# Router products of one more block on TensorE, expert weights split four slots ahead, output scaling on VectorE

## The chip, the cores and the metric

The kernel runs on one core of a Trainium2 chip. The metric is the device time of one execution in microseconds (us), lower is better. In the profile PE is TensorE (PEld its weight loads), DVE is VectorE, ACT is ScalarE, POOL is GpSimd and SP is the engine that only issues transfers.

## The reference

Three layers follow each other on 2304 tokens of 512 features, all in fp32. First comes a linear attention of 4 batches with 8 heads each, which produces the tokens. The second layer is a dense pair of products with a leaky relu, 512 to 2048 and back to 512. The third, where the change lies, sends every token to one of eight experts:

```python
logits = xn @ en.T / tau            # xn, en: rows of x and of expert_emb, normalised
expert_idx = np.argmax(logits, axis=1)
probs = softmax(logits)             # with 1e-9 in the sum
gate_w = probs[np.arange(N), expert_idx]
for e in range(E):
    mask = expert_idx == e
    h = np.maximum(x[mask] @ w1[e], 0.0)      # 512 -> 1024
    out[mask] = gate_w[mask, None] * (h @ w2[e])   # 1024 -> 512
```

## The kernel before

**Precision.** A product in fp32 is made of three passes: each operand is split into a rounded part `hi` (a cast on ScalarE) and the rest `lo` (a subtraction), and hi*hi, hi*lo and lo*hi are added up in PSUM.

**Dense layer.** Tokens are worked in nine blocks of 256 (j = 0 to 8), twice: a first pass with half of the 2048 hidden features, together with the attention, and a second pass (`mm1`, `mm2`) with the other half. After a block's second pass `y_half_b(j)` (L564) adds both halves to `ys` on VectorE, stores the rows, and needs the products of each row with the eight expert embeddings. For j < `J_PE` these are 16 reductions over 512 elements on VectorE (L582, two row tiles by eight experts, with the embeddings `enb` held broadcast in SBUF). For j >= `J_PE`, only j = 8 before, TensorE transposes the rows (L593), ScalarE copies them (L595), and TensorE multiplies them with the embeddings (L601). `route(j)` then picks the expert and counts ranks with many small VectorE operations and four small matmuls (L631, L632).

**Lists.** The tokens of one expert are gathered in tiles of 128. Five early tiles (0 to 4) are listed from the first twelve row tiles, while the dense layer is still running. The late list (`make_list`, `list_ids`, `list_tail`) needs block 8's routing; its VectorE work runs while the early tiles are computed, and its matmuls stand at fixed places of the steps: ranks (L632) at the start of step 2, counts (L680) in step 2, ids (`pp`, L754) in step 3, gates (L781) in step 5.

**Expert steps.** Step i computes tile i in four slots. Slot 0 is the first half of the up product (`up(i, 0)`, L901 to L905), slot 1 the first half of the down product of tile i-1 (`down(i-1, 0)`, L931 to L935) and the transposes of tile i's hidden values (`hT(i, 0)`, L915), slots 2 and 3 the second halves. ScalarE takes the relu of an up product (`hs`, L908) and casts the transposed values (`h`, L918), and `hT` can't start before `hs`. TensorE keeps the written order in all steps. In steps 0 and 1 (`I_ACT`) ScalarE keeps the written order too. Elsewhere a scheduler places the instructions ahead of time by priority and by its own estimate of when each is ready, and each engine then runs them in that fixed order.

**Weights.** An expert's weights are four chunks of 1 MB, c = 0 to 3, each with one buffer `raw[c]`. `split(k)` (L841) makes the pair of slot k: `whi` by two casts of 1024 columns on ScalarE (L856), `wlo` by two subtractions (L858), on VectorE but for the second half of c = 3, and of c = 2 in tiles 0 to 2 (`I_POOL`, `C_POOL`), which go to GpSimd. After it, GpSimd issues the load of the next tile's chunk into `raw[c]` (L816), only where the expert changes. Pair k is split in program order `LEAD` = 2 slots before its use. There is room for six pairs: four in `ring_b` (the room of the dense layer's weights W8 to W15, free as block 8's second product uses them up), one in `xb` (the room of two blocks' inputs) and one in `ring_c` (the room of `enb`, free once the last product on VectorE is done). Which pool a pair takes goes by its place modulo six (L845).

**Output.** `finish(i)` (L937) scales a tile's result by its gate on ScalarE (L940, out of PSUM) and GpSimd scatters the rows to the output (L941). The last two of 25 possible tiles stand under a condition that is not met here: 23 run.

Of the kernel before, what the change touches and what calls it, by code (L numbers as in the profile page):

```python
# [15 lines left out]
AF = mybir.ActivationFunctionType  # L16
ALU = mybir.AluOpType
# [19 lines left out]
N_PLAIN = 23  # L37
BIG = 8192.0
PRIO = 1000
J_PE = 8  # L40
J_UP = 9
W_DVE = ()
N_TOP = 2
# [16 lines left out]
MAN = (mybir.EngineType.PE,)  # L60
ENDS = (0, 1)
TAILS = ((1, 1), (1, 2), (2, 0), (2, 1))
I_POOL = (0, 1, 2)
C_POOL = (2,)


# [1 line left out]
def tile_attention_moe_router_experts(ctx, tc, qT, kT, va, w_phi, moew, emb, embT, tau, ew, out):  # L68
    nc = tc.nc
# [9 lines left out]
    def bc(ap, shape):  # L79
        return ap.to_broadcast(shape)  # L80
# [18 lines left out]
    for i in range(2):  # L99
        for r in range(2):  # L100
            nc.vector.tensor_copy(
                out=wblk[r * D:(r + 1) * D, i, r * F:(r + 1) * F],
                in_=wstk[r * D:(r + 1) * D, i, :].bitcast(F32),
# [373 lines left out]
    def b_load(j):  # L477
# [23 lines left out]
        out=upper, in_=upper, pattern=[[1, P]], compare_op=ALU.is_gt, fill=0.0, base=0, channel_multiplier=-1  # L501
# [4 lines left out]
    def iota_f(shape, pattern, base_, cm, name):  # L506
# [16 lines left out]
        out=lt8, in0=bc(io8.unsqueeze(2), [P, NE, NE]),  # L523
# [40 lines left out]
    def y_half_b(j):  # L564
        yt = ypt.pop(j)
        on_pe = j >= J_PE
        yss = []
# [226 lines left out]
    def gather(i):  # L794
        xgt = m1.tile([P, DM], F32, tag="xgt", name="xgt")
        nc.gpsimd.indirect_dma_start(
            out=xgt, out_offset=None, in_=y_d[0:T_EARLY * P, :] if i < N_EARLY else y_d,
            in_offset=bass.IndirectOffsetOnAxis(ap=lists[i][1], axis=0),
        )
        xgs[i] = xgt  # L800

    def xT(i):
        xgt = xgs.pop(i)
        ps = ps_t.tile([P, DM], F32, tag="t", name="xtp")
        for k in range(4):
            nc.tensor.transpose(ps[:, k * P:(k + 1) * P], xgt[:, k * P:(k + 1) * P], ident)
        x = m1.tile([P, 2, 4, P], F32R, tag="xt", name="xt")
        with tc.high_priority(offset=200):
            nc.scalar.copy(out=x[:, 0], in_=ps)
            nc.vector.tensor_sub(  # L810
                x[:, 1].rearrange("q k t -> q (k t)"), ps, x[:, 0].rearrange("q k t -> q (k t)").bitcast(F32)
            )
        xt[i] = x
# [10 lines left out]
    def load_w(i, c):  # L824
        if i == 0 or i >= N_PLAIN:
            load_rows(i, c)
            return
        if i not in need:
            need[i] = nc.values_load(
                lists[i][2], engines=[mybir.EngineType.Pool], min_val=0, max_val=3 * NE  # L830
            )
        with tc.If(need[i] < NE):
            load_rows(i, c)

    def chunk_of(k):
        i, s = divmod(k, 4)
        return ((i, 0), (i - 1, 2), (i, 1), (i - 1, 3))[s]
# [3 lines left out]
    def split(k):  # L841
        i, c = chunk_of(k)
        if not span[0] <= i < span[1]:
            return
        n = (k - 2 if k > 3 else k // 2) % 6  # L845
        if n == 2:
            pool, tag = xg, "xb"
        elif n == 5:
            pool, tag = ring_c, "W"
        else:  # L850
            pool, tag = ring_b, "W"
        hi = pool.tile([P, 2048], F32R, tag=tag, name="whi")
        lo = pool.tile([P, 2048], F32R, tag=tag, name="wlo")
        for h in range(2):
            hs_ = slice(h * 1024, (h + 1) * 1024)
            nc.scalar.copy(out=hi[:, hs_], in_=raw[c][:, hs_])  # L856
            eng = nc.gpsimd if h == 1 and (c == 3 or (i in I_POOL and c in C_POOL)) else nc.vector
            eng.tensor_sub(lo[:, hs_], raw[c][:, hs_], hi[:, hs_].bitcast(F32))  # L858
        wt_[i, c] = (hi, lo)
        if i + 1 < span[1]:  # L860
            load_w(i + 1, c)
# [60 lines left out]
    yacc = {}  # L922
# [14 lines left out]
    def finish(i):  # L937
        oi, gt = tails[i]
        o = xg.tile([P, DM], F32, tag="w32", name="o", bufs=3)
        nc.scalar.activation(out=o, in_=yacc.pop(i), func=AF.Copy, scale=gt)  # L940
        nc.gpsimd.indirect_dma_start(  # L941
            out=out, out_offset=bass.IndirectOffsetOnAxis(ap=oi, axis=0), in_=o, in_offset=None,
            bounds_check=NTOK - 1, oob_is_err=False,
        )

    LEAD = 2

    def step(i, t0, t1, at):
        live, prev, more = i < t1, i > t0, i + 1 < t1
        at(i, 0)  # L950
        if 4 * i + LEAD > 3:
            split(4 * i + LEAD)
        if more:
            gather(i + 1)
        if live:
            up(i, 0)
        at(i, 1)
        split(4 * i + 1 + LEAD)
        if prev:
            down(i - 1, 0)  # L960
        if live:
            hT(i, 0)
        at(i, 2)
        split(4 * i + 2 + LEAD)
        if live:
            up(i, 1)
        if more:
            xT(i + 1)
        at(i, 3)
        split(4 * i + 3 + LEAD)  # L970
        if prev:
            down(i - 1, 1)
            finish(i - 1)
        if live:
            hT(i, 1)

    def run(t0, t1, at=lambda i, n: None):
        span[:] = [t0, t1]
        for i in range(t0, t1 + 1):
            lead = tc.manual_schedule(engines={mybir.EngineType.Activation}) if i in I_ACT else nullcontext()  # L980
            with lead:
                step(i, t0, t1, at)
# [35 lines left out]
    with tc.If(live_rv > N_PLAIN - N_EARLY):  # L1018
        span[:] = [N_PLAIN, N_TILES]
        gather(N_PLAIN)  # L1020
        for c in range(4):
            load_w(N_PLAIN, c)
        xT(N_PLAIN)
        split(4 * N_PLAIN)
        with tc.manual_schedule(engines=set(MAN)):
            run(N_PLAIN, N_TILES)

# [46 lines left out]
```

## Time and profile before

| | |
|---|---|
| median of 3 runs | 945.04 us (941.79 to 949.37) |
| profiled execution | 945.95 us, span 944.1 us |
| busy: PE, DVE, ACT, POOL | 889.6 (94%), 681.5 (72%), 567.1 (60%), 349.2 (37%) us |
| DMA | 120.67 MB, 128 GB/s over the span |
| stages | attention and first pass to about 415, second pass to 621, expert steps from 616 to 930 |

The span is from the first to the last instruction; the execution's own time is 1.85 us longer. TensorE's matmuls overlap in the records, so a stretch with PE busy throughout can still hide small stalls; the waits are read from the idle time in brackets.

### The profile page before, as it was taken

How to read it: one execution, taken by the hardware profiler on the slowest of the kernel's cores; microseconds unless marked ns; L12 is line 12 of the kernel's file. 1: busy time of each engine (PE TensorE's matmuls, PEld its weight loads, DVE VectorE, ACT ScalarE, POOL GpSimd, SP SyncE). 2: the span in 40 equal slices, each digit the busy share in tenths (PEclk: the TensorE clock that was granted, in tenths of full speed). 3: DMA queues.
4: the chain of work that ended last, by engine and by line, in shares of the span. 5: the costliest groups of instructions: out<-in, count | busy, mean ns of one | idle time of the engine just before them, and what ended most of it. 6: DMA issues, size and time to landing. Idle time of an engine off the chain costs nothing. (4 is left out here: it accounts for less than half of the span.)

```text
span 944.1 us, 18507 instructions
## 1 busy us (share of the span) xinstructions
PE 889.6 (94%) x7104; PEld 758.7 (80%) x7104; DVE 681.5 (72%) x1337; ACT 567.1 (60%) x1032; POOL 349.2 (37%) x269
## 2 busy tenths in 40 slices
PE   7889999999999899879999999997889999999994
PEld 5678888888898788779888889886678887888873
DVE  5676547475654544656888889999998888898860
ACT  5876647485555544753333333476788987888861
POOL 1321203032020321562223334426664576554650
PEclk9999999999999999999999999999899999999997
DMA  8773414223030212872222224401551469311650
GB/s 257 245 236 107 140 38 136 94 72 115 25 114 31 84 67 74 270 261 90 90 91 90 90 90 141 184 34 61 192 194 45 160 209 352 136 41 35 227 187 6
DMA packets 43756, 120.67 MB, mean 128 GB/s; under 512 B 4686, under 2 KB 23246, under 8 KB 36624
## 3 DMA queue, kind: packets, MB, share of 16 engines
q1 hardware_dynamic: 33424, 61.48, 19.8%
q0 software_dynamic: 10160, 57.94, 17.6%
q8 instruction: 57, 0.93, 0.4%
q14 instruction: 35, 0.29, 0.1%
q10 hardware_dynamic: 80, 0.03, 0.0%
HBM read 95.84 MB, written 24.90 MB: 128 GB/s over the span
## 5 line engine op out<-in xcount | busy, mean ns | idle before, releaser
L354 PE MATMUL y<-W,gg 128*128 128x512 f32 x864 | 232.3, 402 | 8.0 <-ACT yt L362 4.6
L858 DVE TENSOR_TENSOR wlo<-raw,whi 128x1024 fp32r<-128x1024 f32 x158 | 200.1, 1299 | 35.3 <-ACT whi L856 35.2
L856 ACT CAST whi<-raw 128x1024 fp32r<-128x1024 f32 x184 | 183.8, 1050 | 48.3 <-DMA raw<-in_ew_dram,lwi 15.1
L354 PEld LDWEIGHTS y<-W,gg 128*128 128x128 f32 x864 | 152.7, 189 | 38.8 <-ACT yt L362 4.8
L333 PE MATMUL h<-xb,W 128*128 128x256 f32 x576 | 164.2, 287 | 3.5 <-DVE g L339 2.8
L334 PE MATMUL h<-xb,W 128*128 128x256 f32 x576 | 162.6, 283 | 0.0
L335 PE MATMUL h<-xb,W 128*128 128x256 f32 x576 | 161.9, 282 | 0.0
L251 POOL PARTITION_ALL_REDUCE qmx<-pr x28 | 55.6, 1992 | 225.1 <-ACT pr L233 222.6
L333 PEld LDWEIGHTS h<-xb,W 128*128 128x128 f32 x576 | 108.7, 190 | 12.0 <-DVE g L339 4.5
L337 ACT ACTIVATE t<-h 128x256 f32<-128x256 f32 x144 | 54.5, 382 | 100.0 <-PE h L335 99.4
L334 PEld LDWEIGHTS h<-xb,W 128*128 128x128 f32 x576 | 109.1, 189 | 5.4 <-DVE xb L293 0.2
L335 PEld LDWEIGHTS h<-xb,W 128*128 128x128 f32 x576 | 109.4, 190 | 0.8
L341 ACT CAST gg<-g 128x256 fp32r<-128x256 f32 x144 | 57.3, 405 | 83.9 <-DVE g L339 82.8
L582 DVE CUSTOM_DVE_ANT_0 jk<-ys,enb 128x512 f32<-128x512 f32 x128 | 105.0, 820 | 1.9
L343 POOL TENSOR_TENSOR gg<-g,gg 128x256 fp32r<-128x256 f32 x72 | 58.8, 820 | 125.0 <-ACT gg L341 120.0
L339 DVE TENSOR_TENSOR g<-h,t 128x256 f32<-128x256 f32 x144 | 59.7, 418 | 59.6 <-ACT t L337 58.5
L858 POOL TENSOR_TENSOR wlo<-raw,whi 128x1024 fp32r<-128x1024 f32 x26 | 65.8, 2533 | 51.8 <-ACT whi L856 51.1
L901 PE MATMUL hps<-whi,xt 128*128 128x512 f32 x184 | 79.0, 429 | 0.0
L931 PE MATMUL yo<-whi,h 128*128 128x512 f32 x184 | 74.6, 406 | 0.0
L902 PE MATMUL hps<-wlo,xt 128*128 128x512 f32 x184 | 74.6, 405 | 0.0
L932 PE MATMUL yo<-wlo,h 128*128 128x512 f32 x184 | 72.7, 395 | 0.0
L322 POOL TENSOR_TENSOR W<-w,W 128x512 fp32r<-128x512 f32 x32 | 43.2, 1361 | 75.5 <-ACT W L321 75.4
(217 smaller groups left out, 1679.7 us busy)
## 6 DMA issues: line engine op xcount, KB each, us to landing
wst<-in_moew_dram SPq DMA_DIRECT2D x32, 512.0 KB, 5.6
qraw<-in_q_dram SPq DMA_DIRECT2D x36, 256.0 KB, 3.1
xs_d<-xb SPq DMA_DIRECT2D x9, 1024.0 KB, 4.5
xb<-xs_d POOLq DMA_DIRECT2D x9, 1024.0 KB, 5.1
kraw<-in_k_dram SPq DMA_DIRECT2D x16, 288.0 KB, 3.4
yp_d<-yt SPq DMA_DIRECT2D x9, 512.0 KB, 2.8
yt<-yp_d SPq DMA_DIRECT2D x9, 512.0 KB, 3.8
y_d<-ys SPq DMA_DIRECT2D x18, 256.0 KB, 2.1
```

The lines of the kernel that those rows point to most:

```text
L333: nc.tensor.matmul(hp, w[:, 0, ks], x[:, 0, k, :], start=(k == 0), stop=False)
L334: nc.tensor.matmul(hp, w[:, 0, ks], x[:, 1, k, :], start=False, stop=False)
L335: nc.tensor.matmul(hp, w[:, 1, ks], x[:, 0, k, :], start=False, stop=(k == 3))
L339: nc.vector.tensor_tensor(out=g, in0=hp, in1=t, op=ALU.max)
L354: nc.tensor.matmul(yps[j][t], gg[:, a, ts], w[:, b, DM:2 * DM], start=(c0 == 0 and a == 0 and b == 0), stop=(c0 == NCH - 1 and a == 1),)
L582: nc.vector.tensor_tensor_reduce(out=jk2, in0=ys, in1=enb[:, e, :], scale=1.0, scalar=0.0, op0=ALU.mult, op1=ALU.add, accum_out=lgr[:, t, ...
L856: nc.scalar.copy(out=hi[:, hs_], in_=raw[c][:, hs_])
L858: eng.tensor_sub(lo[:, hs_], raw[c][:, hs_], hi[:, hs_].bitcast(F32))
L901: nc.tensor.matmul(ps, x[:, 0, k], hi[:, ks], start=(k == 0), stop=False)
L902: nc.tensor.matmul(ps, x[:, 0, k], lo[:, ks], start=False, stop=False)
L931: nc.tensor.matmul(yacc[i], h2[:, 0, k], hi[:, w0], start=(nh == 0 and k == 0), stop=False)
L932: nc.tensor.matmul(yacc[i], h2[:, 0, k], lo[:, w0], start=False, stop=False)
```

## The change

Block 7's products move to TensorE as well (`J_PE` 8 to 7). GpSimd keeps only the second half of c = 3 (`I_POOL` empty). `LEAD` goes from 2 to 4, so that pair k stands two slots earlier in the written order; the pair of slot 2 of the conditional tiles is added ahead of their steps. The pools change places: the pair first in the six now takes `ring_c`, the sixth takes `xb`. `finish` scales on VectorE.

```diff
-J_PE = 8
+J_PE = 7
...
-I_POOL = (0, 1, 2)
+I_POOL = ()
...
         n = (k - 2 if k > 3 else k // 2) % 6
-        if n == 2:
+        if n == 5:
             pool, tag = xg, "xb"
-        elif n == 5:
+        elif n == 0:
             pool, tag = ring_c, "W"
         else:
             pool, tag = ring_b, "W"
...
         o = xg.tile([P, DM], F32, tag="w32", name="o", bufs=3)
-        nc.scalar.activation(out=o, in_=yacc.pop(i), func=AF.Copy, scale=gt)
+        nc.vector.tensor_scalar(out=o, in0=yacc.pop(i), scalar1=gt, scalar2=None, op0=ALU.mult)
...
-    LEAD = 2
+    LEAD = 4
...
         xT(N_PLAIN)
         split(4 * N_PLAIN)
+        split(4 * N_PLAIN + 2)
```

## Rows read from the trace of the kernel before

**Rows 1.** Windows: us; busy time (count) of PE, PEld, DVE, ACT, POOL; PEclk, DMA share, GB/s

```profile
596.00:621.00 25.00, 24.92 (x147) 21.74 (x147) 23.56 (x58) 11.66 (x25) 8.94 (x9) 1.00 0.22 84
621.00:705.00 84.00, 72.27 (x421) 58.70 (x421) 81.93 (x126) 67.25 (x88) 48.03 (x26) 0.92 0.39 135
705.00:912.00 207.00, 205.49 (x986) 167.20 (x984) 172.25 (x164) 177.71 (x228) 121.39 (x72) 1.00 0.45 156
912.00:944.00 32.00, 18.39 (x84) 14.58 (x84) 4.83 (x6) 7.04 (x11) 5.44 (x4) 0.84 0.06 24
```

**Rows 2.** Timeline of PE: start, us, engine, line, op, tiles; in brackets idle before, releaser

```profile
625.92 0.66 PE L915 MATMUL htp<-ident,hs 128*128 128x128 f32 x4 [0.64 <-ACT hs L908]
...
643.86 0.17 PE L632 MATMUL prk<-cum,ones 128*128 128x8 bf16 x1 [1.90 <-DVE cum L627]
...
664.64 1.11 PE L915 MATMUL htp<-ident,hs 128*128 128x128 f32 x4 [6.76 <-ACT hs L908]
...
688.24 1.11 PE L915 MATMUL htp<-ident,hs 128*128 128x128 f32 x4 [2.43 <-ACT hs L908]
```

**Rows 3.** Timeline of PE: one up pass at full rate, one at half rate

```profile
635.18 0.47 PE L901 MATMUL hps<-whi,xt 128*128 128x512 f32 x1
...
638.07 0.60 PE L806 MATMUL xtp<-ident,xgt 128*128 128x128 f32 x4
...
643.89 0.78 PE L901 MATMUL hps<-whi,xt 128*128 128x512 f32 x1
...
648.33 0.18 PE L680 MATMUL cnt<-cum,ones 128*128 128x8 bf16 x1
```

**Rows 4.** Timeline of ACT around the longest wait

```profile
662.10 1.99 ACT L856 CAST whi<-raw 128x1024 fp32r<-128x1024 f32 x2 [7.72 <-DMA raw<-in_ew_dram,ewi]
663.99 0.59 ACT L908 ACTIVATE hs<-hps 128x512 f32<-128x512 f32 x1
```

**Rows 5.** Timeline of DVE and POOL before that transfer was issued

```profile
653.93 1.22 DVE L858 TENSOR_TENSOR wlo<-raw,whi 128x1024 fp32r<-128x1024 f32 x1
...
655.41 1.92 POOL L816 DMA_INDIRECT raw<-in_ew_dram,ewi  x1 [4.51 <-DVE cm L693]
```

**Rows 6.** Timeline: one small DVE operation alone, and beside a half on POOL

```profile
622.50 0.20 DVE L638 TENSOR_TENSOR ge<-rr,thr 128x36 f32<-128x36 f32 x1
...
648.41 2.49 POOL L858 TENSOR_TENSOR wlo<-raw,whi 128x1024 fp32r<-128x1024 f32 x1
648.56 2.41 DVE L638 TENSOR_TENSOR ge<-rr,thr 128x36 f32<-128x36 f32 x1
```

**Rows 7.** Window of line 582 alone: us, DVE busy (16 products with their 16 reads)

```profile
596.00:621.00 25.00, 13.68 (x32) 1.00 0.22 84
```

**Rows 8.** Timeline of PE: block 8's transposes and products

```profile
629.26 1.04 PE L593 MATMUL ytp<-ident,ys 128*128 128x128 f32 x8
...
633.37 1.95 PE L601 MATMUL plg<-ent,yT 128*128 128x8 f32 x16
```

**Rows 9.** Timeline of ACT in step 0, in the written order

```profile
622.91 0.57 ACT L918 CAST h<-htp 128x512 fp32r<-128x512 f32 x1
623.37 1.99 ACT L856 CAST whi<-raw 128x1024 fp32r<-128x1024 f32 x2
625.27 0.59 ACT L908 ACTIVATE hs<-hps 128x512 f32<-128x512 f32 x1
```

**Rows 10.** Groups by form: count | busy us, mean ns | idle before, releasers

```profile
L940 ACT ACTIVATE o<-yo,lgt 128x512 f32<-128x512 f32 x18 | 12.3, 684 | 7.0 <-PE yo L935 7.0
L573 DVE TENSOR_TENSOR ys<-y,yt 128x512 f32<-128x512 f32 x18 | 11.8, 686 | 1.9 <-PE y L354 1.9
L856 ACT CAST whi<-raw 128x1024 fp32r<-128x1024 f32 x184 | 183.8, 1050 | 48.3 <-DMA raw<-in_ew_dram,lwi 15.1 <-PE hps L902 10.5 <-DMA raw<-in_ew_dram,ewi 9.7
```

**Rows 11.** Timeline of DVE and PE: the late list's last part and its matmuls

```profile
675.02 0.52 DVE L739 TENSOR_TENSOR bw<-bw,thr 128x360 bf16<-128x360 bf16 x1
...
675.77 1.05 PE L754 MATMUL pp<-bw,rm 128*128 128x20 bf16 x36
```

## The prediction

> **What bounds the kernel now.** I read the windows first, one for each stage around the change. TensorE is busy for 24.92 of 25 us in the last block and for 205.49 of 207 us in the late expert steps; between them, from 621 to 705, it is busy for 72.27 of 84 us, and its granted clock falls to 0.92 [rows 1]. So TensorE bounds every stage but that one. VectorE is full there (81.93 of 84 us), ScalarE and GpSimd are not. The timeline of TensorE shows what it waits for in that stretch: 0.64, 1.90, 6.76 and 2.43 us, 11.7 us together, three times for the relu of an up product and once for the rank sums [rows 2]. After the longer three it runs at half rate for a while: an up pass takes 2.89 us at full rate and 4.44 us at half, 1.55 us more [rows 3]. That makes 11.7 + 3 x 1.55 = 16.4 us that the stretch could give back.
>
> The longest wait has its cause three engines away. The relu came at 663.99, right behind a pair of casts that had stood 7.72 us waiting for an expert's rows [rows 4]; that relu's product had been ready for long, but ScalarE's order is fixed. I infer from the code that the transfer awaited is the one issued at 655.41, as soon as VectorE had finished with the buffer by its subtraction at 653.93 [rows 5]: from issue to use 6.7 us. VectorE was late since it was full.
>
> **Part 1: block 7's products.** Sixteen products leave VectorE, 13.68 us between 596 and 621 [rows 7]. On TensorE block 8 shows the price: eight transposes 1.04 us, and 635.18 - 633.37 = 1.81 us for the products [rows 3, 8], 2.8 us in all. TensorE has 0.08 us idle there [rows 1], so nothing hides them: **+2.8**. The bounds are 1.8 (transposes partly inside small gaps) and 3.8 (a wait for the copies, on ScalarE, which is half idle). VectorE's relief lies before 621, and what can be moved into it is limited: block 7's routing, and the pair that Part 2 brings forward.
>
> **Part 2: four slots ahead.** Outside steps 0 and 1 I give this nothing: pairs already start when TensorE releases their room (10.5 us of ScalarE's waits before the casts end on L902 [rows 10]), and six pairs of room stay six. Where a step's written split moves, its load on GpSimd's queue moves with it, past a gather or a scatter; an issue holds GpSimd for some 1.9 us [rows 5], and I price that at zero, bounds -2 and +2. In steps 0 and 1 ScalarE keeps the written order, and there it matters. Pair 4 ran at 623.37, behind the first cast of hidden values [rows 9]; now it stands ahead of the first relu, and its room in `ring_b` comes free before 616, since pair 0 takes `ring_c`, which no product holds any more. So one pair is done before the stretch begins. But two pairs (5 and 6) now stand ahead of the relu at 625.27 where one stood, and TensorE already waited for it: **+2.0** for one more pair of casts (1.99 us [rows 9]), bounds 0 and 3.5, the latter with half rate after it. Queued behind are the cast of tile 1's rows and the next transposes.
>
> **Part 3: GpSimd's halves.** When GpSimd subtracts a half (2.49 us), VectorE's small operation beside it takes 2.41 us in place of 0.20 [rows 6]. VectorE does a half itself in 1.22 us [rows 5]. Three halves move; held time saved lies between 0 and 2.2 us for each, since not every operation is held so long. I take 1.7: 3 x (1.7 - 1.2) = 1.5 us of VectorE's time gained. The Trainium skill, SBUF — State Buffer, Who interferes with whom, has GpSimd and a VectorE operation with two SBUF inputs contend for a shared pair of ports, and lets a 2-port operation be blocked for the whole instruction. By that rule all 2.49 us come back each time, 3.8 us, and the sum below would be 2.3 us lower; the row comes near it.
>
> **Part 4: the scale.** 684 ns leave ScalarE and about 686 come to VectorE, by a VectorE operation of the same size out of PSUM [rows 10]. From 705 on VectorE is at 172.25 of 207 us [rows 1], so some 17 more scales, 12 us, fit: 0. At the very end one scale is on the path on either engine: 0. In the full stretch the four scales cost VectorE 2.8 us, the first of them 0.7 before the transfer at 655.41.
>
> **Part 5: the waits.** The rank sums waited 1.90 us because VectorE was held; TensorE now comes 2 us later to them: **-1.9**. The half rate after it moves to the relu of Part 2, no change. For the transfer at 655.41 VectorE is earlier by pair 4 (two halves, 2.4), by block 7's ranks done before 621 (seven operations of some 0.2 us [rows 6], 1.4), by Part 3's 1.5, less 0.7 of the scale: **-4.6** of 6.76 us, bounds 0 and -8.3 with its half rate. The 2.2 us left still cost the half rate, as the 1.90 us did. The wait at 688.24 is of the same kind, behind transfers of the same chain; 4.6 us earlier covers its 2.43 us, and its half rate goes: **-4.0**, bounds 0 and -4.0.
>
> **Sum.** 2.8 + 2.0 - 1.9 - 4.6 - 4.0 = -5.7 us on the profiled execution's own 945.95 us: 940.3. That execution lies 0.9 us above the median, so I expect 939.4, say 940.
>
> **Rivals.** *All the stretch's waits go.* Each needs only a few us of VectorE's lead, and the half rate goes with them: 2.8 - 16.4 = -13.6, 931.4 against the median. For it speaks that the lag is a chain whose start moves by 4.6 us; against it that Part 2 adds to the first wait.
>
> *VectorE sets the pace.* It has 81.93 us of work in 84 [rows 1], and its work changes only by -2.4 - 1.4 - 1.5 + 2.8 = -2.5 us. The late list shows it: its last operation ends at 675.54, and TensorE takes it up at 675.77 [rows 11], so TensorE can't pass that point sooner than VectorE. Then Part 1's 2.8 us eats the 2.5: 945.3. The Trainium skill, Perfetto Trace Analysis, Optimizing Scalar/DVE Operations, advises moving work to ScalarE where VectorE is saturated; Part 4 does the opposite, and by that page this rival would hold. The rows bear out the full VectorE but not that every wait is its work: the longest was order on ScalarE. A variant ends at the same time: the pools' limit of six pairs makes the four slots an empty change in steps 0 and 1 too.
>
> *Slower: transfers awaited in the written order.* ScalarE's waits for late experts' rows are 15.1 us [rows 10], nearly all hidden behind one down pass of 2.9 us between an up product and its transposes. If pairs placed earlier stand ahead of more relus, that cover is used up once a wait passes 0.9 us (2.9 less a pair's 2.0). Half of 15.1 us on the path, with Parts 1 and 2 and no gain in Part 5: 2.8 + 2.0 + 7.5 = +12.3, 957. Against it: outside steps 0 and 1 relus have priority over casts where both are ready.
>
> **How the numbers follow.** A change of 1% (9.45 us) is about what runs from 941.8 to 949.4 can tell from none; under 935.6 is faster, over 954.5 slower. Forecast 0.43, of which 0.08 under 935.6 by Part 5's far bounds. All waits gone 0.24. VectorE's pace or an empty change 0.22, all within 1%. Slower 0.11, of which 0.01 within. So faster 0.32, same 0.58, slower 0.10. The range from 930 to 950 leaves out the slow case and the far end of the fast one. The forecast's own range is 935 to 945.
>
> **What would show it.** Part 1: block 7's transposes in the second pass, and the expert steps starting 2 to 3 us later. Part 2: two pairs of casts between the second squares and the relu after them, and a wait of near 3 us there. Part 3: no 2.4 us ranks or counts on VectorE but beside a half of c = 3. Part 5: the transfer behind 655.41 some 2 us earlier, and the long wait at about 2 us. It would be wrong if the long wait stands as before, if the list's matmuls wait for VectorE, or if new waits appear after 705, where I count none.

## The result: 959.6 us, 1.35% slower

| | before | after |
|---|---|---|
| median (runs) | 945.62 us (6) | 959.57 us (6), 955.86 to 964.08 |
| ratio | | 1.0135, 95% interval 1.0111 to 1.0159 |
| profiled execution, its span | 945.95, 944.1 us | 964.08, 962.4 us |
| first up product of step 0 | 615.68 us | 618.25 us |
| steps 0 to 5 | 94.95 us | 102.90 us |
| steps 6 to 22 | 219.79 us | 227.42 us |

I had predicted 940 us (930 to 950). The profiled execution of after lies 4.5 us above its median, that of before 0.3 us, so the stages show where the time lies, and the ratio how much it is. A stage begins at the first matmul of `up(i, 0)` in TensorE's timeline; the last one ends with the last down product. The spans differ by 18.2 us: 2.6 before the expert steps, 7.9 in steps 0 to 5, 7.6 from step 6 on. The last part is a stage in which I had counted nothing.

Windows of after (fixed in time, while its step 6 begins at 721.15 and that of before at 710.63; us; busy time and count of PE, PEld, DVE, ACT, POOL; PEclk, DMA share, GB/s), to be held against [rows 1]:

```profile
596.00:621.00 25.00, 25.00 (x165) 22.20 (x164) 13.98 (x36) 12.62 (x26) 7.85 (x10) 1.00 0.19 72
621.00:705.00 84.00, 68.59 (x346) 55.17 (x345) 66.36 (x112) 57.09 (x76) 37.23 (x21) 0.90 0.36 121
705.00:912.00 207.00, 201.96 (x996) 162.71 (x995) 185.49 (x179) 161.89 (x204) 120.22 (x67) 0.98 0.41 139
```

VectorE gets its relief before 621 (23.56 to 13.98 us), and from 621 to 705 it is no longer full (81.93 to 66.36). Yet TensorE does less in that stretch, 68.59 us against 72.27. VectorE's longest gap there is a wait for a cast, which stands in ScalarE's order behind a copy of block 8's rows:

```profile
641.47 1.23 DVE L858 TENSOR_TENSOR wlo<-raw,whi 128x1024 fp32r<-128x1024 f32 x1 [7.07 <-ACT whi L856]
```

From 705 on TensorE loses 3.5 us of busy time, some of it still in step 5; before it had hardly any gap there.

TensorE's waits in steps 0 to 5 of after (start, length, line; in brackets the idle time before and the releaser), against [rows 2]:

```profile
630.67 1.10 PE L915 MATMUL htp<-ident,hs 128*128 128x128 f32 x4 [3.02 <-ACT hs L908]
...
653.34 0.19 PE L631 MATMUL prk<-oh,upper 128*128 128x8 bf16 x1 [5.19 <-DVE oh L625]
...
656.27 0.17 PE L632 MATMUL prk<-cum,ones 128*128 128x8 bf16 x1 [2.70 <-DVE cum L627]
...
682.42 0.17 PE L754 MATMUL pp<-bw,rm 128*128 128x20 bf16 x1 [0.98 <-DVE bw L738]
...
695.63 1.12 PE L915 MATMUL htp<-ident,hs 128*128 128x128 f32 x4 [2.82 <-ACT hs L908]
...
712.16 1.51 PE L781 MATMUL pg<-bg,rm 128*128 128x20 bf16 x52 [1.90 <-DVE bg L774]
```

The wait of 6.76 us for a relu is gone. The one of 2.43 us, at the first transposes of step 4, stands: it is 2.82 us now (695.63), behind a cast that awaited a late expert's rows:

```profile
693.09 1.99 ACT L856 CAST whi<-raw 128x1024 fp32r<-128x1024 f32 x2 [3.33 <-DMA raw<-in_ew_dram,lwi]
```

The first relu costs 3.02 us where it cost 0.64, the rank sums 5.19 + 2.70 us where they cost 1.90, and the gates' products of step 5 now wait 1.90 us. Step by step, after takes 2.5 us more than before in step 0, 7.4 more in step 1, 6.6 less in step 2, 1.2 more in step 3, 0.2 in step 4 and 3.2 in step 5. Ahead of the relu that the transposes at 630.67 await ScalarE now has two pairs of casts, where [rows 9] has one:

```profile
625.78 1.98 ACT L856 CAST whi<-raw 128x1024 fp32r<-128x1024 f32 x2
627.66 0.57 ACT L918 CAST h<-htp 128x512 fp32r<-128x512 f32 x1
628.14 1.99 ACT L856 CAST whi<-raw 128x1024 fp32r<-128x1024 f32 x2
630.03 0.59 ACT L908 ACTIVATE hs<-hps 128x512 f32<-128x512 f32 x1
```

Why the rank sums wait stands in VectorE's timeline, in the four us ahead of them:

```profile
648.68 0.74 DVE L940 TENSOR_SCALAR o<-yo,egt 128x512 f32<-128x512 f32 x1
649.34 0.16 DVE L624 TENSOR_REDUCE m<-wt 128x2 f32<-128x16 f32 x1
649.41 3.78 DVE L858 TENSOR_TENSOR wlo<-raw,whi 128x1024 fp32r<-128x1024 f32 x2
653.12 0.16 DVE L625 TENSOR_TENSOR oh<-wt,m 128x16 bf16<-128x16 f32 x1
653.20 2.35 DVE L858 TENSOR_TENSOR wlo<-raw,whi 128x1024 fp32r<-128x1024 f32 x2
655.47 0.68 DVE L919 TENSOR_TENSOR h<-htp,h 128x512 fp32r<-128x512 f32 x1
656.07 0.34 DVE L627 TENSOR_TENSOR cum<-cum,oh 128x8 bf16<-128x8 bf16 x2
```

Block 8's routing is a row of operations of some 0.2 us, each dependent on the one before. In VectorE's fixed order pairs of subtractions stand between them, and the scale stands there too. The four slots pulled the pairs ahead: with two slots and all else as in after (a1, below) the rank sums have no such wait. Not all of the delay arises here: against the first up product the routing's first operation (L606) comes 3.7 us later than before, after a longer step 0, and its last (oh, L625) 9.3 us later. Two subtractions take 2.35 us; the two at 649.41 took 3.78, with GpSimd's half from 647.71 to 650.97 beside them:

```profile
647.71 3.26 POOL L858 TENSOR_TENSOR wlo<-raw,whi 128x1024 fp32r<-128x1024 f32 x1 [1.16 <-ACT whi L856]
```

### The profile page after: what moved, and what is told of

It reads as the page before. It is cut to its first block, busy times and chain, and to the rows that moved or that the text cites. A ratio compares the mean times of both kernels' runs of the same rounds, so it can differ in the third digit from the quotient of the medians.

```text
span 962.4 us, 18517 instructions
## 1 busy us (share of the span) xinstructions
PE 899.5 (93%) x7128; PEld 764.4 (79%) x7128; DVE 685.1 (71%) x1331; ACT 554.6 (58%) x1011; POOL 348.8 (36%) x266
## 5 line engine op out<-in xcount | busy, mean ns | idle before, releaser
L858 DVE TENSOR_TENSOR wlo<-raw,whi 128x1024 fp32r<-128x1024 f32 x161 | 214.3, 1364 | 37.9 <-ACT whi L856 37.3
L582 DVE CUSTOM_DVE_ANT_0 jk<-ys,enb 128x512 f32<-128x512 f32 x112 | 91.5, 817 | 1.8
L858 POOL TENSOR_TENSOR wlo<-raw,whi 128x1024 fp32r<-128x1024 f32 x23 | 62.3, 2710 | 47.0 <-ACT whi L856 40.6
```

The source lines that it names most:

```text
L582: nc.vector.tensor_tensor_reduce(out=jk2, in0=ys, in1=enb[:, e, :], scale=1.0, scalar=0.0, op0=ALU.mult, op1=ALU.add, accum_out=lgr[:, t, ...
```

## The experiments

Each was timed in five rounds beside the kernel before, whose medians were 946.9 to 947.7 us in the five sets. The stages, in us, are from each profile; "late load" is the time from the first up product to the issue of the first load that the late list names (`lwi`).

| kernel | median | ratio (95%) | steps 0 to 5 | 6 to 22 | late load |
|---|---|---|---|---|---|
| before (set 1) | 947.43 | | 94.95 | 219.79 | 52.7 |
| after | 959.57 | 1.0135 | 102.90 | 227.42 | 55.9 |
| a1_lead2 | 965.55 | 1.0169 (1.0132, 1.0206) | 107.88 | 226.11 | 67.3 |
| a2_scale_act | 949.50 | 1.0016 (0.9987, 1.0044) | 92.99 | 222.71 | 52.4 |
| b1_lead4 | 958.73 | 1.0112 (1.0073, 1.0152) | 103.07 | 222.23 | 58.7 |
| b2_scale_dve | 955.70 | 1.0087 (1.0061, 1.0112) | 100.19 | 226.49 | 56.9 |
| b3_jpe7 | 951.83 | 1.0035 (1.0009, 1.0062) | 97.30 | 222.10 | 52.7 |
| b4_ipool | 953.28 | 1.0069 (1.0043, 1.0094) | 102.15 | 220.27 | 60.4 |
| c1_nohalf_act | 944.42 | 0.9967 (0.9941, 0.9992) | 94.84 | 218.27 | 52.7 |
| c2_nohalf_dve | 948.31 | 1.0009 (0.9984, 1.0035) | 100.29 | 219.31 | 56.9 |
| a4_lead2_act | 960.63 | 1.0139 (1.0109, 1.0168) | 109.00 | 223.39 | 63.9 |
| a5_act_free | 944.46 | 0.9973 (0.9950, 0.9997) | 91.54 | 223.13 | 50.1 |
| a6_tails | 953.67 | 1.0089 (1.0054, 1.0125) | 102.04 | 220.15 | 60.8 |
| b6_dve_pos | 959.45 | 1.0137 (1.0109, 1.0165) | 104.61 | 225.03 | 56.9 |
| d1_dve_order | 955.36 | 1.0080 (1.0053, 1.0108) | 98.00 | 223.88 | 56.9 |
| d2_lead2_order | 960.33 | 1.0117 (1.0088, 1.0146) | 105.38 | 223.80 | 63.8 |
| d4_lead4_order | 957.62 | 1.0094 (1.0070, 1.0119) | 103.80 | 225.89 | 58.7 |
| d5_cand | 948.61 | 1.0016 (0.9985, 1.0047) | 92.77 | 219.73 | 52.4 |
| e1_after_list | 955.91 | 1.0076 (1.0044, 1.0107) | 94.81 | 225.39 | 51.8 |
| e2_cand_list | 945.86 | 0.9989 (0.9966, 1.0013) | 91.57 | 221.32 | 51.6 |

**Set 1: the scale against the written order.** Theory W: four slots in ScalarE's written order cost the time, in steps 0 and 1. Theory S: the scale on VectorE costs it, in the late steps. a1 is the changed kernel with the first edit (and without the pair added for the conditional tiles), a2 with the second; b1 and b2 are the kernel before with the reverse of each.

```diff
-    LEAD = 4
+    LEAD = 2
...
-        nc.vector.tensor_scalar(out=o, in0=yacc.pop(i), scalar1=gt, scalar2=None, op0=ALU.mult)
+        nc.scalar.activation(out=o, in_=yacc.pop(i), func=AF.Copy, scale=gt)
```

> The changed kernel with LEAD back at 2, all else as changed. Theory W (the four slots put casts of weights ahead of the relus in the written order of steps 0 and 1, and that costs most of the 14 us): 951 to 953 us, with no wait of 3 us before the second transposes of step 0 and no wait of 5 us for the rank sums. Theory S (the scale on VectorE costs most, in the late steps): no more than 2 us below the changed kernel, 958.

> The changed kernel with the scale back on ScalarE, all else as changed. Theory S: 952 to 954 us, the late steps (from the first up product of step 6 to the last down product) 219 to 221 us as before, against 227 in the changed kernel. Theory W: 958 to 959, the waits in steps 0 to 2 as in the changed kernel.

> The kernel before with LEAD 4 alone. Theory W: 952 to 954 us, with the wait of some 3 us for the relu in step 0. Theory S: 946 to 947. If the four slots need the other pools to work, above 954.

> The kernel before with the scale on VectorE alone. Theory S: 951 to 953 us, with a lower half of the casts ahead of the rest of the gathered rows' split in the late steps. Theory W: 946 to 947.

With the scale back on ScalarE 10.1 us of after's 959.6 go (11.3 by the two ratios, 1.19% of 946); alone, in the kernel before, it costs 8.3 us (955.7 against 947.4). S holds, and by more than it asked, since steps 0 to 5 pay too (9.9 and 5.2 us), not only the late ones (4.7 and 6.7). W fails in a1, which is not faster (its interval overlaps after's). In b1, four slots alone cost 11.3 us. So the parts don't add: four slots cost time in the kernel before and save it beside the other parts (a4 against a2, below). At 958.7 b1 also lies above 954, the sign set down for four slots that need the other pools. No run exchanges the pools alone, or the pools and the slots and nothing else, so that rival stays untested.

**Set 2: why idle time on VectorE was no room.** In the late steps of after and b2 VectorE's subtractions (L858) are longer. Groups of VectorE from 710 to 912 us (count, busy us, mean ns, idle before), first before, then a2, then b2:

```profile
L858 DVE TENSOR_TENSOR wlo<-raw,whi 128x1024 fp32r<-128x1024 f32 x112 | 141.6, 1299 | 29.8 <-ACT whi L856 29.8
```

```profile
L858 DVE TENSOR_TENSOR wlo<-raw,whi 128x1024 fp32r<-128x1024 f32 x112 | 141.7, 1300 | 31.2 <-ACT whi L856 27.5 <-PE hps L905 2.2 <-PE hps L902 1.3
```

```profile
L858 DVE TENSOR_TENSOR wlo<-raw,whi 128x1024 fp32r<-128x1024 f32 x110 | 151.8, 1418 | 13.5 <-ACT whi L856 13.4
...
L940 DVE TENSOR_SCALAR o<-yo,lgt 128x512 f32<-128x512 f32 x15 | 11.0, 737 | 0.0
...
L940 DVE TENSOR_SCALAR o<-yo,egt 128x512 f32<-128x512 f32 x1 | 0.8, 751 | 0.1
```

In b2 sixteen scales add 11.8 us, and two subtractions fewer take 10.2 us more. Sorted by whether a half of c = 3 ran on GpSimd at the same time, 25 subtractions of before took 1590 ns beside one and 87 took 1216 alone; in b2 24 took 2160 and 86 took 1211. One step of b2 shows what that does. VectorE and GpSimd:

```profile
902.34 5.02 DVE L858 TENSOR_TENSOR wlo<-raw,whi 128x1024 fp32r<-128x1024 f32 x2
907.28 0.68 DVE L810 TENSOR_TENSOR xt<-xtp,xt 128x512 fp32r<-128x512 f32 x1
907.88 0.73 DVE L940 TENSOR_SCALAR o<-yo,lgt 128x512 f32<-128x512 f32 x1
```

```profile
902.72 2.41 POOL L858 TENSOR_TENSOR wlo<-raw,whi 128x1024 fp32r<-128x1024 f32 x1
```

and TensorE:

```profile
907.28 0.40 PE L902 MATMUL hps<-wlo,xt 128*128 128x512 f32 x1
908.01 1.21 PE L905 MATMUL hps<-whi,xt 128*128 128x512 f32 x4 [0.33 <-DVE xt L810]
```

Two subtractions take 5.02 us instead of 2.35, the low half of tile 22's rows (L810) comes late, and TensorE's up product stands. That wait is the smaller part: in b2's late steps TensorE waits 0.8 us for low halves and 3.5 us for relus, against none and 1.5 us before. The longest of these follows from the same place. The scale at 907.88 is late, GpSimd's scatter waits for it, the next load stands behind the scatter, and a cast and the relu behind it wait for a load (that it is this one is inferred from the order):

```profile
908.90 1.74 POOL L941 DMA_INDIRECT out_dram<-o,loi  x1 [1.78 <-DVE o L940]
911.69 1.83 POOL L816 DMA_INDIRECT raw<-in_ew_dram,lwi  x1 [1.05 <-issue]
918.08 1.99 ACT L856 CAST whi<-raw 128x1024 fp32r<-128x1024 f32 x2 [3.93 <-DMA raw<-in_ew_dram,lwi]
920.62 0.66 PE L915 MATMUL htp<-ident,hs 128*128 128x128 f32 x4 [2.15 <-ACT hs L908]
```

Theory C: the scale costs by this. Rival R: it costs by its place in the order. c1 takes the halves out of the kernel before, c2 out of b2, with this edit (`down`'s second product reads `lw`), from tile 5 on; their results lack that part of the correction. b3 has `J_PE` at 7 and b4 `I_POOL` empty, each as in the change and alone.

```diff
-            eng.tensor_sub(lo[:, hs_], raw[c][:, hs_], hi[:, hs_].bitcast(F32))
+            if c != 3 or h != 1 or i <= 4:
+                eng.tensor_sub(lo[:, hs_], raw[c][:, hs_], hi[:, hs_].bitcast(F32))
...
+            lw = hi if nh == 1 and k > 1 and i > 4 else lo
```

> The kernel before, scale on ScalarE, but from tile 5 on GpSimd's half of c = 3 is left out (the product that would read it reads hi in its place, so the rest of half a chunk is left out; TensorE's work is the same). Control for the next one. Both theories: steps 6 to 22 take 218 to 220 us (before 219.8), 943 to 948 in all.

> The one above (GpSimd's halves of c = 3 left out from tile 5 on) with the scale on VectorE. Theory C: in the late steps the scale costs time because VectorE, fuller by 0.74 us a step, now has its subtractions beside GpSimd's halves and is held by them (24 subtractions took 2160 ns beside a half, 86 took 1211 ns alone). Without the halves steps 6 to 22 stay within 1.5 us of the control, where they were 6.7 us longer with them; the early steps keep their +5: 4 to 7 us above the control. Rival R: the scale costs by its place in VectorE's order, 0.74 us each step ahead of the subtractions that TensorE waits for, halves or not: steps 6 to 22 5 to 7 us longer than the control, 10 to 13 us in all.

> The kernel before with block 7's products on TensorE (J_PE 7) and nothing else. By Part 1 of the prediction: +2.8 us on TensorE before the expert steps (up(0,0) at 618.5 against 615.7), and part of it given back in steps 0 to 5 because VectorE is relieved by 13.7 us before 621: 946 to 951. Rival: the relief lets the late list run earlier and takes the waits of 6.8 and 2.4 us in steps 2 and 4 away: 938 to 944. Steps 6 to 22 unchanged at 219.8 us by both.

> The kernel before with GpSimd's three halves of c = 2 in tiles 0 to 2 given to VectorE (I_POOL empty) and nothing else. By Part 3 (1.5 us of VectorE's time gained in steps 0 to 3): 944 to 947. Theory C (while GpSimd subtracts a half, VectorE's operation beside it is held for all of it): up to 3.8 us gained in VectorE's full stretch, and with it the 6.8 us wait shortened: 940 to 945. Rival: three halves of 1.2 us more on an engine that is full there: 948 to 951. Steps 6 to 22 unchanged at 219.8 us.

Without the halves the scale adds 1.0 us to steps 6 to 22 (218.27 to 219.31) in place of 6.7. The group of c2 has as many scales and no lengthening:

```profile
L859 DVE TENSOR_TENSOR wlo<-raw,whi 128x1024 fp32r<-128x1024 f32 x112 | 132.5, 1218 | 22.7 <-ACT whi L856 21.4 <-PE xtp L806 1.4
...
L942 DVE TENSOR_SCALAR o<-yo,lgt 128x512 f32<-128x512 f32 x15 | 11.3, 750 | 1.7
```

C holds for the late steps. One reserve: without the halves GpSimd's queue is also freer and the chunk earlier, and no run parts these from the holding. The early steps keep their 5.4 us. b3 costs 4.9 us by the medians: its first up product is 1.8 us later, step 4 and steps 13 to 15 take 2.3 and 2.2 us more, and VectorE's relief brings nothing in sight; the waits of 6.8 and 2.4 us stand, the latter at 3.7. b4 has the wrong sign: 6.4 us slower. There the ids' products wait 9.5 us, since on VectorE a subtraction whose cast awaits a transfer stands between two operations of the late list; VectorE, and ScalarE's cast:

```profile
676.18 0.52 DVE L735 TENSOR_TENSOR bw<-key,slot 128x360 bf16<-128x360 f32 x1
676.63 0.18 DVE L541 RECIPROCAL nr12r<-nr12s 128x6 f32<-128x6 f32 x1
682.33 1.22 DVE L858 TENSOR_TENSOR wlo<-raw,whi 128x1024 fp32r<-128x1024 f32 x1 [5.52 <-ACT whi L856]
683.47 0.31 DVE L738 TENSOR_SCALAR bw<-bw,pos 128x360 bf16<-128x360 bf16 x1
```

```profile
681.25 1.99 ACT L856 CAST whi<-raw 128x1024 fp32r<-128x1024 f32 x2 [5.18 <-DMA raw<-in_ew_dram,lwi]
```

The ids' products wait 9.4 us in b1, 6.9 in b2 and 5.3 in a1, and not at all in before and a2.

**Set 3: is that one place the cost of the early steps?** Theory L says so.

a4 has the edits of a1 and a2 together. a5 is a2 with the first edit, a6 is a2 with the second, b6 is b2 with the third.

```diff
-I_ACT = (0, 1)
+I_ACT = ()
...
-TAILS = ((1, 1), (1, 2), (2, 0), (2, 1))
+TAILS = ((1, 1), (1, 2), (2, 1), (2, 2))
...
-POS = (3, 3)
+POS = (4, 0)
```

> The changed kernel with two of its parts undone: LEAD 2 and the scale on ScalarE (block 7's products on TensorE, GpSimd's halves and the pools stay as changed). If the parts' effects add: 959.6 + 6.0 (LEAD 2, a1) - 10.1 (scale, a2) = 955.5. Theory L: steps 0 to 5 are decided by whether a subtraction that awaits a transfer stands between two dependent operations of the late list (L735 and L738) on VectorE; it did with LEAD 2 and the scale on VectorE (5.3 us), so this run falls into two cases: with that wait 952 to 957, without it 944 to 948; the trace shows which.

> The changed kernel with the scale on ScalarE and I_ACT empty: ScalarE's order in steps 0 and 1 is the scheduler's and not the written one. Theory W: the written order costs there (the transposes of step 0 wait 3.0 us for a relu behind two pairs of casts, the rank sums 4.0 and 1.0 us behind the subtractions that follow late): the relus go ahead of the casts, 942 to 946. Rival: the scheduler's own order has pairs awaiting transfers ahead of relus as well, 949 to 956.

> The changed kernel with the scale on ScalarE and the rank sums and counts of block 8 one slot later in TensorE's order (TAILS (2,1) and (2,2) for (2,0) and (2,1)). TensorE then has an up pass of 2.9 us to do before it waits for VectorE's ranks: the waits of 4.0 and 1.0 us fall to about 2 and the half rate after them may go, 945 to 947.5. Rival: VectorE paces the list, and what is gained comes back as a wait of the ids' products (L754): 949 to 952.

> The kernel before with the scale on VectorE and the ids' products (L754) at the start of step 4 in place of slot 3 of step 3, some 4 us later in TensorE's order. Theory L (their wait of 6.9 us for the list's operation behind a subtraction that awaits a transfer is the scale's cost in the early steps): the wait falls to about 3 us, 951 to 953. Rival: the scale costs there because VectorE is full, and the time returns at the next product that waits for it: 955 to 957. If the gather behind the ids comes too late for tile 5's transposes: over 957.

a4 has the wait, at 13.6 us, and is slower than either case forecast, 11.1 us over a2: beside the other parts four slots do earn their place. In a6 the rank sums' first wait falls from 4.03 us in a2 to 1.35, their second stays (0.96, 0.98), and 12.6 us come back at the ids' products: its rival's mechanism, though 953.7 us is above its range. In b6 the ids' wait falls from 6.9 to 0.5 us, and 4.8 and 1.1 us come back at the gates' products (L781): its rival's mechanism too. But its 959.5 us lie above 957, the sign set down for a late gather, and the gather is 0.44 us late at tile 5's transposes; what the rest is stays open. a5 is W's one success: with ScalarE's order free, 944.5 us, 0.27% under the kernel before with an interval just clear of 1, the fastest of those that do the whole work.

**Set 4: that order alone.** The subtractions of tile 5's first chunk are put behind the list's last operation, where they stand in the kernel before.

```diff
-        nc.vector.tensor_tensor(
+        listed[0] = nc.vector.tensor_tensor(
             out=bw[:, :, 2, :], in0=bw[:, :, 0, :], in1=bc(thr[:, 0:T].unsqueeze(2), [P, T, E]), op=ALU.mult
...
-            eng.tensor_sub(lo[:, hs_], raw[c][:, hs_], hi[:, hs_].bitcast(F32))
+            with tc.issue_after(listed[0].ins) if k == 20 else nullcontext():
+                eng.tensor_sub(lo[:, hs_], raw[c][:, hs_], hi[:, hs_].bitcast(F32))
```

> The kernel before with the scale on VectorE (as b2), and one order added: the two subtractions of tile 5's first chunk (slot 20, the first transfer that the late list itself names) stand behind the list's last operation (L739 in the kernel before) on VectorE, where in b2 they stood ahead of L738 and waited for their transfer. Theory L: the 6.9 us wait of the ids' products goes, steps 0 to 5 fall from 100.2 to 95 to 97 us (a wait like that of 2.4 us in step 4 before may return), steps 6 to 22 stay at 226.5: 950 to 952.5. Rival: VectorE is full there and the time comes back at the next product that waits for it, as with the later ids (b6): 955 to 958.

> a4 (the changed kernel with LEAD 2 and the scale on ScalarE) with the same order added. There the wait was 13.6 us. Theory L: it goes, 944 to 949. Rival: VectorE's fullness, 955 or more.

> The kernel before with LEAD 4 (as b1) and the same order added. Theory L: of b1's 10.6 us the 9.4 us wait of step 3 goes (a few of them return in step 4), 949 to 953; what is left above before is the price of LEAD 4 itself, 2.5 us in each of steps 0 and 1 and 2.4 in the late steps by b1's trace. Rival: LEAD 4 costs by pairs awaited in the written order, order of the list or not: 956 to 960.

> A candidate: the kernel before with GpSimd's three halves of c = 2 on VectorE (Part 3, as b4), ScalarE's order in steps 0 and 1 the scheduler's (I_ACT empty, which helped a5), and the same order added. If each helps by itself: b4's 9.5 us wait goes and step 2's 6.8 us wait with it, 938 to 943. Rival: the free order brings late waits for transfers as in a5 (3.3 us in steps 6 to 22): 944 to 948.

Theory L falls. In d1 the wait drops to 1.5 us and steps 0 to 5 by 2.2 of 6.9; the time is b2's. In d2 it drops from 13.6 to 4.0 us and the time stays. In d4 it stands at 8.5 us: the list's operation now waits behind another one, L539, which awaits ScalarE behind the same transfer. So that place is where the lag shows, not where it comes from. d5 beats nothing.

**Set 5: the list ahead of the subtractions.** In all the traces above the length of steps 0 to 5 goes with the moment of the first late load (in the table: 50 to 53 us and 91.5 to 97.3; 56 to 61 and 98 to 104.6; 64 to 67 and 105 to 109). Theory T took that moment for the cause. The subtractions of slots 13 to 16 are put behind the list's expert numbers (`wi`, L711): the edit of set 4 with `listed[0]` taken there, and this condition.

```diff
+            with tc.issue_after(listed[0].ins) if k in (13, 14, 15, 16) else nullcontext():
```

> The changed kernel, whole, with one order added on VectorE: the subtractions of slots 13 to 16 stand behind the late list's expert numbers (L711 of the changed kernel), so that the list's dependent operations run one behind the other and not each behind a subtraction. Theory T: steps 0 to 5 last as long as it takes until the late list names the first late expert and its load is issued (55.9 us after the first up product here, 52.7 in the kernel before; in 16 kernels the longer of the two goes with the longer of the other). The issue comes at 46 to 49 us, steps 0 to 5 fall from 102.9 to 94 to 97 us, steps 6 to 22 stay at 227: 950 to 954. Rival: VectorE has no room, the subtractions held back are late for step 3 in its place: 957 or more.

> A candidate to beat both kernels: the changed kernel with the scale on ScalarE and I_ACT empty (a5, issue at 50.1 us, steps 0 to 5 in 91.5) and the same order added. Theory T: issue at 43 to 46, steps 0 to 5 in 86 to 89 us, steps 6 to 22 as in a5: 939 to 942. Rival: in a5 the list is no longer what steps 0 to 5 wait for (its longest wait is 3.0 us in step 5, for the gates' operations): 943 to 946.

e1 takes steps 0 to 5 from 102.90 to 94.81 us, as forecast, and the median from 959.6 to 955.9 (the ratio from 1.0135 to 1.0076), so 8.1 us of those steps in single profiles are 3.7 us by the medians and 5.6 by the ratios. The forecast of the total, and that of the issue, were too low: the list names its experts at 660.52, 38.9 us after the first up product (54.4 in after), but the load goes out only at 51.8, behind an earlier expert's load and GpSimd's half, which took 6.87 us beside five subtractions:

```profile
662.02 6.87 POOL L860 TENSOR_TENSOR wlo<-raw,whi 128x1024 fp32r<-128x1024 f32 x1 [4.25 <-ACT whi L857]
669.04 1.83 POOL L817 DMA_INDIRECT raw<-in_ew_dram,ewi  x1
673.43 1.01 POOL L817 DMA_INDIRECT raw<-in_ew_dram,lwi  x1 [2.56 <-issue]
```

```profile
660.52 0.22 DVE L712 SCALAR_TENSOR_TENSOR lwi<-same,p4c 128x80 int32<-128x80 f32 x1
660.68 0.29 DVE L731 TENSOR_TENSOR tm<-oh,off 128x144 f32<-128x144 bf16 x1
660.89 5.75 DVE L860 TENSOR_TENSOR wlo<-raw,whi 128x1024 fp32r<-128x1024 f32 x5
```

Most of e1's gain lies in step 1, 6.2 us (24.88 to 18.68): the rank sums wait 2.9 us instead of 7.9. Of the two pairs around the one-hot in after, slot 13's (653.20) now stands behind the list; slot 12's (649.41), which the edit doesn't name, comes behind the rank sums in the order that the scheduler made anew. So it is shown that the order of VectorE's small operations among the subtractions costs 8 us of steps 0 to 5 in the changed kernel, of which 4 to 6 count in its time; that the late load is what the rest waits for is not. e2 has a5's steps 0 to 5 and no more: its rival.

## Why the prediction was wrong

**Part 4, the scale at 0**, is the step that failed: 10.1 us in the changed kernel, 8.3 alone. I counted VectorE's idle time from 705 on (207 less 172.25) as room for 12 us of scales. About half of that idle time lay beside GpSimd's halves of c = 3: from 710 to 912 sixteen of 2.47 us, 39.6 in all, for 18.4 of which VectorE stood idle in before and for 9.7 in b2. [Rows 6] had shown what an operation of VectorE beside a half costs; I used it in Part 3 and left it out here. A fuller VectorE meets more of each half, and a subtraction beside one takes 2160 ns in place of 1590. "In the full stretch the four scales cost VectorE 2.8 us" was the right work, but they stand between dependent operations that TensorE waits for: 5 to 10 us.

**Part 3** had the sign wrong. The holding that it counts on stands in [rows 6], and 1.5 us may be gained there, but b4, alone in the kernel before, reached the late list's expert numbers 7.8 us later (58.97 after the first up product against 51.21) and lost 6.4 us. What counts is not VectorE's sum but which of its operations stand ahead of the list.

**Part 5** held in one term of three: the wait of 6.76 us went (I had left 2.2 of it). That of 2.43 us, for which I took off 4.0 with its half rate, stayed at 2.82. And "TensorE now comes 2 us later to them: -1.9" took the routing as fixed. It came 9.3 us later itself (oh at 34.9 us after the first up product against 25.5), and the rank sums waited 7.9 us. Of the 9.3 us 3.7 are TensorE's own delay, passed on with block 8's products; the rest are the operations in between. I asked whether VectorE is earlier at one transfer, and not what the pairs brought forward stand ahead of. With the scale on ScalarE (a2) steps 0 to 5 gained 2.0 us, of the 8.5 to which Parts 2 and 5 add up there (2.0 - 1.9 - 4.6 - 4.0). Of the signs of being wrong two came: the list's matmuls wait for VectorE, and from step 6 on the relu waits grew from 1.5 us to 4.8. A smaller slip: I priced the half rate at 1.55 us after each wait, from the row after the rank sums; after the two relu waits it cost 1.1 and 1.2 (up passes of 3.96 and 4.09 us against 2.89), so the stretch could give back 15.6 us and not 16.4.

**Parts 1 and 2 in step 0** were right: the steps start 2.6 us later (forecast 2.8; over ten profiles each the mean start is 614.4 us with `J_PE` at 8 and 617.5 at 7), and the first relu waits 3.02 us (forecast "near 3"), step 0 growing from 10.71 to 13.17. In a2 steps 6 to 22 take 2.9 us more, nearly all of it in steps 13 and 14, where a relu stands behind casts that await a transfer. That this is Part 2 is not shown: with two slots b3, the products alone, takes 2.3 us more in steps 6 to 22, with the same wait in step 13, and a4 3.6. It is my slower rival's mechanism, at 2.9 us instead of 7.5; 957 was near the result by luck, for a reason that explains a fifth of it at most.

**VectorE sets the pace** named the right engine at the wrong price. The Trainium skill, Perfetto Trace Analysis, Optimizing Scalar/DVE Operations, says that where VectorE is saturated it may make sense to hand some of its work to ScalarE; a2 agrees, where the scale moved back to ScalarE gives 10.1 us. By its busy share (172 of 207 us) VectorE did not look saturated. The Trainium skill, SBUF — State Buffer, Who interferes with whom, has a VectorE operation with two SBUF inputs contend with a GpSimd operation that reads SBUF, and the order of issue decide which of the two is blocked: 2160 against 1211 ns here agrees, and so does the half of 6.87 us in e1, the same thing the other way. I had applied that rule to three of GpSimd's 26 halves.

What stays open: why four slots cost 11 us in the kernel before and save 11 beside the other parts (with the scale on ScalarE; with it on VectorE, a1 against after, 3 to 6 us, not clear of noise), and what the pools have to do with it. The traces show where (the late load 6.0 us later in b1 than in before, 11.5 us earlier in a2 than in a4), not the rule by which the scheduler's order falls so.

## What to carry to other kernels

Idle time of an engine is room only if nothing that holds it runs in it: subtract the other engine's instructions that contend before pricing added work at nothing. Where a chain of short dependent operations shares an in-order engine with long ones, price a moved instruction by what it stands ahead of, and not by its length. And time one part of a change at a time: here one cost more than all of them together were to give.

## What the runs showed of the hardware that I had not expected

The holding goes both ways: a half on GpSimd, 2.40 us at its shortest in e1, took 6.87 us beside five subtractions, which kept their 1.15 us each (e1, above). A scale out of PSUM took 737 to 752 ns on VectorE and 684 on ScalarE [rows 10]. The work ahead of the expert steps varies by several us between single profiles: the first up product came between 610.2 (b6) and 618.0 us (d1) in ten with `J_PE` 8, and those two kernels differ only behind it. So single profiles are compared by stages.
